# A scale from row sums on ScalarE, and three of six gates on ScalarE and GpSimd, at the seam of a fused block kernel

## The chip, the cores and the metric

The kernel runs on one core of a Trainium2 chip. A core has five engines with a queue of instructions each: TensorE (PE in the profile; its weight loads are PEld), VectorE (DVE), ScalarE (ACT), GpSimd (POOL) and SyncE (SP, which here issues the DMAs). Each engine takes its own queue in order; engines wait for each other through semaphores. The metric is the device time of one execution in microseconds; less is better.

## The reference

Three blocks follow each other on a batch of 4 sequences of 448 rows and 768 features. The cut below keeps what is computed.

```python
# attention with a sigmoid in place of the softmax; 12 heads of 64
scores = scale * q @ k.T - log(S)
x = sigmoid(scores) @ v                      # (4, 448, 768)

# Fourier mixing over rows and features, then a normed two-layer network
u = x + real(fft(fft(x, axis=1), axis=2))
un = (u - mean(u)) / sqrt(var(u) + 1e-6)
x = u + relu(un @ w_ch1) @ w_ch2             # 768 -> 3072 -> 768

# the convolution block: a causal 5-tap convolution per feature gates a projection
gate = sigmoid(sum_k conv_w[k] * x[:, s - 4 + k, :])
out = (gate * (x @ w_val)) @ w_out
```

## The kernel before

Features lie on the 128 partitions in 6 tiles, the 448 rows along the free axis; `acc[b]` holds one batch entry as 128 x 6 x (4 + 448) numbers in fp32 (four zeros of padding for the convolution). In the order of instructions the four are called `acc_90`, `acc_92`, `acc_94` and `acc_96`.

A product of fp32 matrices is made of three fp16 products: each operand is scaled by a power of two and split into a high and a low half. The scale needs the largest magnitude of a whole tensor, over all partitions. `peak` finds it: `peak_row` (lines 107 to 113) reduces a 128 x n tile of partial results to a column on DVE and spreads it to a diagonal `pd`; `peak_spread` (L118) lets PE multiply that by ones, which copies the column to all partitions; `peak_max` (L123) reduces it on DVE; `pow2` and `scaled` (L152 to L160) make the scale of it. **L118 is a matmul in PE's queue like any other: if `pd` isn't there, all of PE's later work waits.**

The code is a set of Python generators. What is recorded between two `yield`s goes to the engines' queues at that place of the program, and nothing is moved afterwards; so the place in the program is the place in each queue. PE's main work calls `background()` between pieces, which takes some steps of each list of side work: `wq` (weights: load, split into halves; then `prep_x2`), `lq`, `fq` (norms and the Fourier part), `gq` (`first_gates`).

The stages: (1) attention, 96 slots `t`, 24 for each batch entry (`r` counts them), with the weights of group 0 and the Fourier part and norm of earlier entries beside it. `amax_v` takes the largest magnitude of a tile of v on DVE, `peak_v` and `scale_v` make the scale that `fourier(b)` needs. (2) The two-layer network in 8 groups of 384 hidden features; block n is group n // 4 and batch entry n % 4. `up(n)` is 54 matmuls into PSUM tiles `ps_s` (two of them), which ACT (`hh`, L737) and DVE (`hl`, L739) evict; `down(n)` is 6 x 9 matmuls into `ps_m` tiles (four of them, taken in turn, L118's too), which DVE adds into `acc[b]` (L757). The blocks run up(n+1), down(n), up(n+2), and so on; the last are up(30), down(29), up(31), down(30), down(31). After down(28) `acc[0]` is final, and so on to `acc[3]` after down(31). (3) The convolution block: `prep_x2(b)` scales and splits `acc[b]` to fp16 halves `xs` (L795 on ACT, L797 on DVE), `first_gates` makes the six gates of entry 0 ahead of time, the other gates are made in the loop; `value` (L907) and `project` (L932) are 18 matmuls each.

Weights of a later block are loaded in halves: `HALF_AT` says at which group each of the four loads (`wv` twice, `wo` twice) is put in `wq`; `constants()` loads the convolution's taps `cw` behind them, and `prep_x2(0)` stands in `wq` behind that.

## Time and profile before

| what | value |
|---|---|
| time, median of 3 runs | 1113.61 us (1111.94 to 1113.67) |
| time of the profiled execution | 1113.55 us |
| its span in the trace | 1111.8 us |
| PE busy | 1066.1 us, 96% of the span |
| DVE, ACT, POOL busy | 756.1, 427.7 and 191.1 us |
| share of PE in the chain that ended last | 76%, DVE 16% |
| PE waiting at L118 | 19.6 us in 7 waits |

What lies around the span is 1113.55 - 1111.8 = 1.75 us. PE is the engine that sets the time wherever it is busy; the table is to be read for where it isn't. A slice of the page's second part is 27.8 us long: PE's busy digit falls below 8 in two slices only, the 35th and 36th of 40, where the granted clock falls too. That is the seam between the two-layer network and the convolution block.

### The profile page before, as it was taken

To read this page: it belongs to the slowest core of one execution; us is meant where nothing else is said; L and a number is where in the kernel's file an instruction comes from. 1 tells how busy PE (TensorE), PEld (TensorE's weight loads), DVE (VectorE), ACT (ScalarE), POOL (GpSimd) and SP (SyncE) were. 2 spreads that over 40 slices of the span, in tenths; PEclk is the share of its full clock that TensorE was granted. 3 is DMA by queue.
4 is the path that set the end of the run, shared out by engine and by line. 5 is a ranking of instruction groups with operands and counts; after the bars stand their busy time and mean duration, and the time that the engine had idled before them with its cause. 6 is when DMAs were issued, how large, how long until landed. Compare 5 with 4: busy or idle time off the path is not lost.

```text
span 1111.8 us, 15303 instructions
## 1 busy us (share of the span) xinstructions
PE 1066.1 (96%) x5616; PEld 550.7 (50%) x5616; DVE 756.1 (68%) x2154; ACT 427.7 (38%) x654; POOL 191.1 (17%) x171
## 2 busy tenths in 40 slices
PE   8899998989899999999999999999999967999998
PEld 4345453546455555555555555555555533555554
DVE  2866999697884676657676765676765679775530
ACT  5675656633232233333423233333233322343321
POOL 3322323331311111111101111110111100000000
PEclk9999999999999999999999999999999978999999
DMA  6723433011111322222333321233321100000001
GB/s 212 211 79 92 122 98 86 10 44 44 30 43 43 86 72 69 73 63 68 85 86 86 81 67 39 72 85 86 87 73 40 32 1 0 1 34 34 34 34 67
DMA packets 34780, 74.13 MB, mean 67 GB/s; under 512 B 3940, under 2 KB 11920, under 8 KB 34704
## 3 DMA queue, kind: packets, MB, share of 16 engines
q1 hardware_dynamic: 34704, 73.15, 23.2%
q8 instruction: 44, 0.72, 0.3%
q14 instruction: 32, 0.26, 0.1%
HBM read 67.46 MB, written 5.51 MB: 66 GB/s over the span
## 4 chain that ended last, share of the span: by engine, by line
PE 76%; DVE 16%; DMA 3%; ACT 3%; issue 1%; POOL 1%; SPq 0%; ACTq 0%; DVEq 0%; POOLq 0%
PE ps_s L730 26%; PE ps_m L753 26%; PE ps_m L932 7%; PE ps_m L907 7%; DMA w<-w1d 3%; PE ps_m L466 2%; PE ps_m L381 2%; PE ps_s L356 2%; PE ps_m L483 1%; DVE gp L820 1%; DVE wf L195 1%; DVE wf L198 1%; DVE xm L105 1%; DVE acc L757 1%; DVE wabs L190 1%
## 5 line engine op out<-in xcount | busy, mean ns | idle before, releaser
L730 PE MATMUL ps_s<-un,w1hi 128*128 128x448 f16 x1152 | 316.6, 357 | 3.5 <-DVE hl L739 3.5
L753 PE MATMUL ps_m<-hh,w2hi 128*128 128x448 f16 x576 | 205.1, 356 | 1.3 <-DVE acc L757 1.2
L730 PE MATMUL ps_s<-un,w1lo 128*128 128x448 f16 x576 | 205.5, 357 | 0.0
L753 PE MATMUL ps_m<-hl,w2hi 128*128 128x448 f16 x576 | 204.9, 356 | 0.0
L753 PE MATMUL ps_m<-hh,w2lo 128*128 128x448 f16 x576 | 204.7, 355 | 0.0
L730 PEld LDWEIGHTS <-w1hi 128*128 128x128 f16 x1152 | 113.5, 99 | 111.0 <-issue 8.8
L753 PEld LDWEIGHTS <-w2hi 128*128 128x128 f16 x1152 | 113.3, 99 | 108.5 <-issue 6.0
L757 DVE SCALAR_TENSOR_TENSOR acc<-ps_m,rg,acc 128x448 f32<-128x448 f32 x192 | 129.1, 678 | 41.8 <-PE ps_m L753 41.7
L179 ACT ACTIVATE wabs<-w 128x384 f32<-128x384 f32 (+1 forms) x109 | 58.4, 548 | 213.0 <-DMA w<-w2d 78.8
L739 DVE SCALAR_TENSOR_TENSOR hl<-ps_s,hh 128x896 f16<-128x896 f32 x64 | 54.6, 854 | 93.0 <-ACT hh L737 92.9
L190 DVE TENSOR_SCALAR_CACHE_REDUCE wabs<-wabs 128x192 f32<-128x192 f32 (+1 forms) x234 | 74.6, 353 | 35.9 <-ACT wabs L179 35.1
L369 ACT ACTIVATE sg<-ps_s,logb 128x896 f32<-128x896 f32 x96 | 86.3, 913 | 26.7 <-PE ps_s L356 22.4
L737 ACT ACTIVATE hh<-ps_s 128x896 f16<-128x896 f32 x64 | 46.2, 722 | 110.4 <-PE ps_s L730 110.4
L730 PEld LDWEIGHTS <-w1lo 128*128 128x128 f16 x576 | 56.9, 99 | 54.1 <-issue 2.5
L753 PEld LDWEIGHTS <-w2lo 128*128 128x128 f16 x576 | 56.8, 99 | 53.8 <-issue 2.0
L198 DVE SCALAR_TENSOR_TENSOR wf<-w,wf 128x192 int32<-128x192 int32 (+1 forms) x234 | 78.1, 371 | 0.3
L907 PE MATMUL ps_m<-xs,wvhi 128*128 128x448 f16 x288 | 78.0, 353 | 0.0
L195 DVE SCALAR_TENSOR_TENSOR wf<-w,wf 128x192 int32<-128x192 int32 (+1 forms) x234 | 77.0, 366 | 0.4
L192 DVE TENSOR_SCALAR wf<-wabs 128x192 int32<-128x192 int32 (+1 forms) x234 | 55.4, 275 | 31.7 <-POOL w1lo L231 12.7
L381 PE MATMUL ps_m<-sg,v 128*64 128x448 f32 x288 | 69.8, 564 | 0.0
L804 DVE SCALAR_TENSOR_TENSOR gp<-acc,cw,gp 128x448 f32<-128x448 f32 x72 | 49.3, 685 | 25.0 <-ACT gp L802 23.1
L932 PE MATMUL ps_m<-gh,wolo 128*128 128x448 f16 x144 | 50.8, 352 | 0.0
(187 smaller groups left out, 1398.4 us busy)
## 6 DMA issues: line engine op xcount, KB each, us to landing
w<-w1d SPq DMA_DIRECT2D x42, 384.0 KB
w<-w2d SPq DMA_DIRECT2D x42, 384.0 KB
k<-kd SPq DMA_DIRECT2D x24, 256.0 KB
v<-vd SPq DMA_DIRECT2D x24, 256.0 KB
q<-qd SPq DMA_DIRECT2D x24, 224.0 KB
out<-o SPq DMA_DIRECT2D x24, 224.0 KB
w<-wvd SPq DMA_DIRECT2D x12, 384.0 KB
w<-wod SPq DMA_DIRECT2D x12, 384.0 KB
```

The lines of the kernel that those rows point to most:

```text
L179: A.activation(out=wa, in_=z[:, :, 1].bitcast(F32), func=AF.Abs)
L190: V.tensor_scalar(out=a, in0=a, scalar1=LEAST, scalar2=None, op0=ALU.max, op1=ALU.max, accum_out=m[:, i:i + 1])
L192: V.tensor_scalar(out=f.bitcast(I32), in0=a.bitcast(I32), scalar1=0x07FFFFFF, scalar2=3, op0=ALU.bitwise_and, op1=ALU.logical_shift_left)
L195: V.scalar_tensor_tensor(out=f.bitcast(I32), in0=lo, scalar=29, in1=f.bitcast(I32), op0=ALU.logical_shift_right, op1=ALU.bitwise_or)
L198: V.scalar_tensor_tensor(out=f.bitcast(I32), in0=hi, scalar=-0x40000000, in1=f.bitcast(I32), op0=ALU.bitwise_and, op1=ALU.bitwise_or)
L369: A.activation(out=sg[:, :n], in_=sc.pop(t)[:, :n, :S], func=AF.Sigmoid, scale=1.0 / math.sqrt(D), bias=logb)
L381: nc.tensor.matmul(p[hs, :S], v[:, s, hs], a[:, h], start=(s == 0), stop=False)
L730: nc.tensor.matmul(p[:, i, :S], w[:, k, fs], u[:, k], start=(m == 0), stop=(m == 17))
L753: nc.tensor.matmul(p[:, :S], w[:, f, js], hh[f // 2][k][:, f % 2], start=(m == 0), stop=(m == 3 * FC - 1))
L757: V.scalar_tensor_tensor(out=acc[b][:, j, PAD:], in0=p[:, :S], scalar=rg, in1=acc[b][:, j, PAD:], op0=ALU.mult, op1=ALU.add)
L907: nc.tensor.matmul(p[:, :S], w[:, k, js], u[:, k], start=(n == 0), stop=(n == 17))
L932: nc.tensor.matmul(p[:, :S], w[:, k, js], gs[b, k][i], start=(n == 0), stop=(n == 17))
```

## The change

- `prep_x2`: the six DVE reductions to the largest magnitude (L105) are replaced by two ACT instructions (`Abs` over 3 x 448 elements each) whose accumulator gives the sum of magnitudes of a row. Their elementwise output goes to the place of the low halves, which L797 later overwrites. The scale's exponent `X2_EXP` goes from 12 to 14. `peak` now waits four steps between `peak_row` and L118, one step after it.
- `first_gates`: the gates are made in pairs (0,3), (1,4), (2,5). The first of a pair is made as before (ACT product, four DVE multiply-adds); of the second, ACT makes all five products (the last four into `gt`) and POOL adds them. The sigmoids come a pair later (`gate_ends`). `gq` gets one step of each `background()`, not two.
- The second half of `wo` is loaded from group 6 on, not 7, and `constants()` stands behind it in group 6.
- In attention, `amax_v` is called one tile ahead, and the three steps of `peak_v` stand at r = 19, 21 and 22 of the same entry, not at r = 23 and at 0 and 1 of the next. The last entry's steps after the loop are gone.
- The peak of the weights of group 0 waits four and two steps, not two and two.

```diff
-X2_EXP = 12
+X2_EXP = 14
-HALF_AT = (1, 3, 5, 7)
+HALF_AT = (1, 3, 5, 6)
...
-    def peak(m, nm, wait):
+    def peak(m, nm, wait, after=1):
         d = peak_row(m, nm)
         for _ in range(wait):
             yield
         p = peak_spread(d)
-        for _ in range(wait):
+        for _ in range(after):
             yield
         return peak_max(p, nm)
...
-        g = yield from (peak(m, nm, 2) if step == WCOLS else peak_pool(m, nm))
+        g = yield from (peak(m, nm, 4, 2) if step == WCOLS else peak_pool(m, nm))
...
-        if t % 4 == 2:
-            amax_v(b, r // 4)
-        if r == 23:
+        if t == 0:
+            amax_v(0, 0)
+        if t % 4 == 2 and t // 4 + 1 < NPAIR:
+            amax_v(*divmod(t // 4 + 1, NT))
+        if r == 19:
             peak_v(b, 0)
-        if b and r == 0:
-            peak_v(b - 1, 1)
-        if b and r == 1:
-            peak_v(b - 1, 2)
-            scale_v(b - 1)
+        if r == 21:
+            peak_v(b, 1)
+        if r == 22:
+            peak_v(b, 2)
+            scale_v(b)
...
-    peak_v(B - 1, 1)
     drain()
     finish(wq)
-    peak_v(B - 1, 2)
-    scale_v(B - 1)
...
     def prep_x2(b):
         xs = acc[b][:, :, PAD:]
-        m = keep.tile([128, NT], F32, tag="xm", bufs=2, name="xm")
-        for j in range(NT):
-            amax(xs[:, j], m, j)
-            if j % 2:
-                yield
-        g = yield from peak(m, "x2", 1)
+        xs2 = homes[b].tile([128, NT, 2 * S], F16, tag=f"un{b}", name="xs")
+        xh, xl = xs2[:, :, :S], xs2[:, :, S:]
+        m = keep.tile([128, 2], F32, tag="xm", bufs=2, name="xm")
+        for h in range(2):
+            hh = slice(3 * h, 3 * h + 3)
+            A.activation(out=xl[:, hh], in_=xs[:, hh], func=AF.Abs, accum_out=m[:, h:h + 1])
+            yield
+        yield
+        g = yield from peak(m, "x2", 4)
...
     def first_gates():
...
-        for j in range(NT):
-            gp = tt[:, j] if j < 4 else tw[:, (j - 4) * S:(j - 3) * S]
-            A.activation(out=gp, in_=acc[0][:, j, 0:S], func=AF.Copy, scale=cw[:, j, 0:1])
+        for pair in range(3):
+            js = pair, pair + 3
+            gp = tt[:, pair], tw[:, pair * S:(pair + 1) * S] if pair < 2 else tt[:, 3]
+            for j, g in zip(js, gp):
+                A.activation(out=g, in_=acc[0][:, j, 0:S], func=AF.Copy, scale=cw[:, j, 0:1])
             yield
             for k in range(1, 5):
-                V.scalar_tensor_tensor(out=gp, in0=acc[0][:, j, k:k + S], scalar=cw[:, j, k:k + 1], in1=gp, op0=ALU.mult, op1=ALU.add)
-                if k % 2 == 0:
-                    yield
-            for _ in range(3):
+                j, g = js[0], gp[0]
+                V.scalar_tensor_tensor(out=g, in0=acc[0][:, j, k:k + S], scalar=cw[:, j, k:k + 1], in1=g, op0=ALU.mult, op1=ALU.add)
+                j, g = js[1], gp[1]
+                A.activation(out=tp[:, n % 5], in_=acc[0][:, j, k:k + S], func=AF.Copy, scale=cw[:, j, k:k + 1])
+                P.tensor_tensor(out=g, in0=g, in1=tp[:, n % 5], op=ALU.add)
+                n += 1
                 yield
-            A.activation(out=gp, in_=gp, func=AF.Sigmoid)
-            gps[0, j] = gp
+            late.append((js, gp))
+            if pair:
+                gate_ends()
...
-        step(gq, 2)
+        step(gq)
...
-            if g == NG - 1:
+            if g == NG - 2:
                 wq.append(constants())
```

**The first peak of the seam, DVE and ACT.** DVE before, from the last of the constants to the first scale of `xs`; it stands in DVE's queue beside the evictions of down(29), and L118 follows on PE after 9 matmuls of up(31):

```order
L777 TENSOR_TENSOR evo_8459<-em,woe 128x1
L105 TENSOR_REDUCE xm<-acc_90 128x1 x2
L820 SCALAR_TENSOR_TENSOR gp<-acc_90,cw,gp 128x448 x2
L757 SCALAR_TENSOR_TENSOR acc_92<-ps_m,rg,acc_92 128x448
L105 TENSOR_REDUCE xm<-acc_90 128x1 x4
L820 SCALAR_TENSOR_TENSOR gp<-acc_90,cw,gp 128x448 x2
L110 TENSOR_REDUCE x2t<-xm 128x1
L112 TENSOR_SCALAR pd<-eye,x2t 128x128
L123 TENSOR_REDUCE x2g<-ps_m 128x1
```

DVE now, in the same place of the program's logic, which is one block and a half earlier; L118 follows on PE after 18 matmuls of down(29):

```order
L738 SCALAR_TENSOR_TENSOR hl<-ps_s,hh 128x896
L198 SCALAR_TENSOR_TENSOR cw<-w_8342,cw 128x30
L768 TENSOR_TENSOR em<-wve 128x1
...
L825 SCALAR_TENSOR_TENSOR gp<-acc_90,cw,gp 128x448
L738 SCALAR_TENSOR_TENSOR hl<-ps_s,hh 128x448
L110 TENSOR_REDUCE x2t<-xm 128x1
L112 TENSOR_SCALAR pd<-eye,x2t 128x128
L825 SCALAR_TENSOR_TENSOR gp<-acc_90,cw,gp 128x448
L756 SCALAR_TENSOR_TENSOR acc_92<-ps_m,rg,acc_92 128x448
L825 SCALAR_TENSOR_TENSOR gp<-acc_90,cw,gp 128x448
L756 SCALAR_TENSOR_TENSOR acc_92<-ps_m,rg,acc_92 128x448
```

ACT now, from the eviction of up(30) to the sigmoids of the first pair:

```order
L736 ACTIVATE hh<-ps_s 128x896
L821 ACTIVATE gp<-acc_90,cw 128x448 x2
L787 ACTIVATE xs,xm<-acc_90 128x3x448 x2
L827 ACTIVATE gt<-acc_90,cw 128x448
L736 ACTIVATE hh<-ps_s 128x448
L827 ACTIVATE gt<-acc_90,cw 128x448 x3
L795 ACTIVATE xs<-acc_90,sx 128x3x448 x2
L821 ACTIVATE gp<-acc_90,cw 128x448 x2
L827 ACTIVATE gt<-acc_90,cw 128x448 x3
L787 ACTIVATE xs,xm<-acc_92 128x3x448 x2
L827 ACTIVATE gt<-acc_90,cw 128x448
L840 ACTIVATE gp<-gp 128x448 x2
```

The six reductions are gone from DVE, and the magnitudes stand in ACT's queue behind the eviction of up(30) and the first products, ahead of the second `hh` of up(30). Four DVE multiply-adds of each pair are left, one between two evictions; POOL's queue has twelve `L828 TENSOR_TENSOR gp<-gp,gt` at its end and nothing beside them.

**The second peak and the evictions of down(30), DVE.** Before, around the same instructions for `acc[1]`:

```order
L105 TENSOR_REDUCE xm<-acc_92 128x1 x4
L110 TENSOR_REDUCE x2t<-xm 128x1
L112 TENSOR_SCALAR pd<-eye,x2t 128x128
L820 SCALAR_TENSOR_TENSOR gp<-acc_90,cw,gp 128x448 x2
...
L797 SCALAR_TENSOR_TENSOR xs<-acc_92,sx,xs 128x3x448
L820 SCALAR_TENSOR_TENSOR gp<-acc_90,cw,gp 128x448 x2
L757 SCALAR_TENSOR_TENSOR acc_94<-ps_m,rg,acc_94 128x448
L797 SCALAR_TENSOR_TENSOR xs<-acc_92,sx,xs 128x3x448
```

Now:

```order
L110 TENSOR_REDUCE x2t<-xm 128x1
L112 TENSOR_SCALAR pd<-eye,x2t 128x128
L825 SCALAR_TENSOR_TENSOR gp<-acc_90,cw,gp 128x448
L738 SCALAR_TENSOR_TENSOR hl<-ps_s,hh 128x896
...
L797 SCALAR_TENSOR_TENSOR xs<-acc_92,sx,xs 128x3x448
L825 SCALAR_TENSOR_TENSOR gp<-acc_90,cw,gp 128x448
L738 SCALAR_TENSOR_TENSOR hl<-ps_s,hh 128x448
L797 SCALAR_TENSOR_TENSOR xs<-acc_92,sx,xs 128x3x448
L825 SCALAR_TENSOR_TENSOR gp<-acc_90,cw,gp 128x448
L756 SCALAR_TENSOR_TENSOR acc_94<-ps_m,rg,acc_94 128x448 x6
```

All six evictions of down(30) now stand behind both L797 of entry 1 and the last of the gates' multiply-adds. L118 follows on PE after 36 matmuls of up(31).

**The end of attention, DVE.** Before, from the last norm of entry 1 to the first eviction of the network's first block:

```order
L617 TENSOR_TENSOR un<-tt,un 128x2x448
L399 TENSOR_TENSOR pm<-acc_96 128x448 x2
L123 TENSOR_REDUCE vg<-ps_m 128x1
L152 TENSOR_SCALAR ve<-vg 128x1
...
L426 TENSOR_TENSOR pm<-acc_96 128x448 x2
L190 TENSOR_SCALAR wabs,wm<-wabs 128x192 x2
L192 TENSOR_SCALAR wf<-wabs 128x192 x2
L430 TENSOR_TENSOR pm<-pm 128x3x223 x2
```

Now:

```order
L123 TENSOR_REDUCE vg<-ps_m 128x1
L152 TENSOR_SCALAR ve<-vg 128x1
...
L617 TENSOR_TENSOR un<-tt,un 128x2x448
L399 TENSOR_TENSOR pm<-acc_96 128x448 x2
L426 TENSOR_TENSOR pm<-acc_96 128x448 x2
L430 TENSOR_TENSOR pm<-pm 128x3x223 x2
L190 TENSOR_SCALAR wabs,wm<-wabs 128x192 x2
L192 TENSOR_SCALAR wf<-wabs 128x192 x2
```

The scale of v's last entry and the last norm of entry 1 stand ahead of the work that follows attention; on SP the DMAs of the Fourier part (L551, L408) now stand ahead of the weight loads, where before they stood behind them.

## Rows read from the trace of the kernel before

**Rows 1.** Stretches: start:end, length, then busy time (x instructions) of PE, PEld, DVE, ACT, POOL, PE's granted clock, DMA.
```profile
225.00:330.00 105.00, 94.09 (x504) 53.03 (x503) 91.75 (x240) 33.23 (x48) 29.77 (x24) 0.95 0.14 39
330.00:870.00 540.00, 539.25 (x2852) 278.85 (x2850) 355.03 (x1289) 174.96 (x280) 86.45 (x80) 1.00 0.27 72
870.00:945.00 75.00, 59.61 (x273) 28.83 (x272) 57.43 (x118) 23.30 (x31) 5.53 (x5) 0.86 0.00 1
```

**Rows 2.** PE's waits in the whole span: us in total, times, longest.
```profile
PE ps_m L118 <- DVE pd L112: 19.6, 7, 5.2
PE ps_s L730 <- DVE hl L739: 3.5, 1, 3.5
```

**Rows 3.** The chain that ended last, at up(30): start, us, engine, line.
```profile
868.75 10.21 PE ps_s L730 x54
```

**Rows 4.** Timeline of PE in the seam: start, us, instruction, [idle before <- releaser].
```profile
895.69 0.47 PE L118 MATMUL ps_m<-pd,ones_r 128*128 128x128 f32 x1 [4.82 <-DVE pd L112]
910.05 0.47 PE L118 MATMUL ps_m<-pd,ones_r 128*128 128x128 f32 x1 [4.80 <-DVE pd L112]
935.89 0.47 PE L118 MATMUL ps_m<-pd,ones_r 128*128 128x128 f32 x1 [5.22 <-DVE pd L112]
943.95 0.54 PE L907 MATMUL ps_m<-xs,wvhi 128*128 128x448 f16 x2
```

**Rows 5.** Timeline of DVE in the seam.
```profile
891.74 2.19 DVE L105 TENSOR_REDUCE xm<-acc 128x1 f32<-128x448 f32 x4
896.21 0.29 DVE L123 TENSOR_REDUCE x2g<-ps_m 128x1 f32<-128x128 f32 x1 [0.57 <-PE ps_m L118]
906.29 1.08 DVE L739 SCALAR_TENSOR_TENSOR hl<-ps_s,hh 128x896 f16<-128x896 f32 x1
909.91 1.40 DVE L820 SCALAR_TENSOR_TENSOR gp<-acc,cw,gp 128x448 f32<-128x448 f32 x2
920.44 0.68 DVE L757 SCALAR_TENSOR_TENSOR acc<-ps_m,rg,acc 128x448 f32<-128x448 f32 x1
940.53 3.14 DVE L797 SCALAR_TENSOR_TENSOR xs<-acc,sx,xs 128x1344 f16<-128x1344 f32 x2
```

**Rows 6.** Timeline of ACT in the seam.
```profile
897.29 2.72 ACT L795 ACTIVATE xs<-acc,sx 128x1344 f16<-128x1344 f32 x2 [9.46 <-DVE sx L160]
903.58 0.92 ACT L737 ACTIVATE hh<-ps_s 128x896 f16<-128x896 f32 x1 [2.54 <-PE ps_s L730]
926.50 0.58 ACT L825 ACTIVATE gp<-gp 128x448 f32<-128x448 f32 x1 [4.80 <-DVE gp L820]
926.98 0.65 ACT L817 ACTIVATE gp<-acc,cw 128x448 f32<-128x448 f32 x1
```

**Rows 7.** Timeline of POOL at the end of attention.
```profile
239.22 1.45 POOL L418 TENSOR_TENSOR pm<-pm 128x339 f32<-128x339 f32 x1 [0.79 <-DVE pm L430]
241.61 1.24 POOL L565 TENSOR_TENSOR tt<-tt,acc 128x448 f32<-128x448 f32 x1
```

**Rows 8.** Timeline of DVE at the end of attention.
```profile
230.15 1.08 DVE L617 TENSOR_TENSOR un<-tt,un 128x896 f16<-128x896 f32 x1
233.17 0.28 DVE L123 TENSOR_REDUCE vg<-ps_m 128x1 f32<-128x128 f32 x1
234.19 1.15 DVE L426 TENSOR_TENSOR pm<-acc 128x448 f32<-128x448 f32 x2
239.83 2.03 DVE L195 SCALAR_TENSOR_TENSOR wf<-w,wf 128x192 int32<-128x192 int32 x2
250.65 0.62 DVE L195 SCALAR_TENSOR_TENSOR wf<-w,wf 128x192 int32<-128x192 int32 x2
```

**Rows 9.** Two stretches of 2 us, columns as in the first group.
```profile
54.00:56.00 2.00, 0.87 (x3) 0.41 (x3) 1.93 (x7) 0.00 (x0) 0.00 (x0) 1.00 0.43 121
248.00:250.00 2.00, 2.00 (x7) 0.79 (x6) 1.63 (x8) 1.02 (x3) 0.00 (x0) 0.50 0.40 155
```

**Rows 10.** Timeline of PE in attention and at its end.
```profile
55.13 0.33 PE L118 MATMUL ps_m<-pd,ones_r 128*128 128x128 f32 x1 [2.52 <-DVE pd L112]
247.37 0.91 PE L730 MATMUL ps_s<-un,w1hi 128*128 128x448 f16 x2 [3.45 <-DVE hl L739]
```

More of the change, by code (lines that the diff above doesn't have):

```diff
@@ L782, in prep_x2 @@
         xs = acc[b][:, :, PAD:]
-        m = keep.tile([128, NT], F32, tag="xm", bufs=2, name="xm")
-        for j in range(NT):
-            amax(xs[:, j], m, j)
-            if j % 2:
-                yield
-        g = yield from peak(m, "x2", 1)
+        xs2 = homes[b].tile([128, NT, 2 * S], F16, tag=f"un{b}", name="xs")
[7 more added lines that the diff above has]
+        g = yield from peak(m, "x2", 4)
         e, i = pow2(g, "x2")
         sx = scaled(i, 2.0 ** X2_EXP, "sx")
-        xs2 = homes[b].tile([128, NT, 2 * S], F16, tag=f"un{b}", name="xs")
-        xh, xl = xs2[:, :, :S], xs2[:, :, S:]
         for h in range(2):
@@ L812, in first_gates, with gate_ends @@
         tw = wp.tile([128, NT, FG], F16, tag="w1hi", bufs=1, name="gp").rearrange("p a b -> p (a b)").bitcast(F32)
+        tp = wp.tile([128, 5, S], F32, tag="wf", bufs=1, name="gt")
+        n = 0
         while len(evo) < 2:
             yield
-        for j in range(NT):
-            gp = tt[:, j] if j < 4 else tw[:, (j - 4) * S:(j - 3) * S]
-            A.activation(out=gp, in_=acc[0][:, j, 0:S], func=AF.Copy, scale=cw[:, j, 0:1])
+        for pair in range(3):
[3 more added lines that the diff above has]
+                A.activation(out=g, in_=acc[0][:, j, 0:S], func=AF.Copy, scale=cw[:, j, 0:1])
             yield
             for k in range(1, 5):
-                V.scalar_tensor_tensor(out=gp, in0=acc[0][:, j, k:k + S], scalar=cw[:, j, k:k + 1], in1=gp, op0=ALU.mult, op1=ALU.add)
-                if k % 2 == 0:
-                    yield
-            for _ in range(3):
-                yield
-            A.activation(out=gp, in_=gp, func=AF.Sigmoid)
-            gps[0, j] = gp
+                j, g = js[0], gp[0]
[4 more added lines that the diff above has]
+                n += 1
+                yield
+            late.append((js, gp))
+            if pair:
+                gate_ends()
+    late = []
+    def gate_ends():
+        js, gp = late.pop(0)
+        for j, g in zip(js, gp):
+            A.activation(out=g, in_=g, func=AF.Sigmoid)
+            gps[0, j] = g
     NBLK = NG * B
@@ L889, in body @@
         step(gq)
+    gate_ends()
     wst.close()
```

## The prediction

> **What bounds the kernel now.** I read the busy time by stretches first: it tells where TensorE is the bound and where not. From 330 to 870 us PE is busy 539.25 of 540 us at a granted clock of 1.00, so nothing that only shortens other engines' work there can pay. From 870 to 945 it is busy 59.61 of 75, from 225 to 330 94.09 of 105 [rows 1]. PE's waits then say for what: 19.6 us in seven waits at L118, and one of 3.5 at L730 [rows 2]. The timeline has three of the seven in the seam, 4.82, 4.80 and 5.22, together 14.84 [rows 4]; 4.76 lie in attention.
>
> The seam in one sum: 54 matmuls of `up` take 10.21 [rows 3], 0.189 each, and a `down` has as many. From the start of up(30) at 868.75 [rows 3] to the first L907 at 943.95 [rows 4] there are five such blocks, 51.05 us. The stretch is 75.20 long, so 24.15 are lost: 14.84 in the three waits, 9.31 around them. Most of those 9.31 I put down to the clock, granted 0.86 in the mean [rows 1]. A wait of 3.45 at 247.37 [rows 10] was followed by two microseconds at 0.50, the 1.2 GHz level; one of 2.52 at 55.13 [rows 10] left the clock at 1.00 [rows 9]. A wait above some 3 us is thus paid more than once, one below 2.5 once.
>
> Why L118 waits: `pd` comes from DVE, whose queue holds six reductions of 0.55 each (2.19 for four), the gates' multiply-adds of 0.70 (1.40 for two) and evictions of 0.68 [rows 5], while PE comes to L118 only nine to 45 matmuls after the block before.
>
> **The change part by part: the seam.** Off DVE: three times six reductions, 18 x 0.55 = 9.9 us, and 12 of 24 multiply-adds, 12 x 0.70 = 8.4. On ACT: six `Abs`, and twelve more products at 0.48 from start to start [rows 6], 5.8. No row of before has an activation with an accumulator. L795 reads and writes as many elements in 1.36 (2.72 for two) [rows 6]: that is the lower bound, twice it the upper. I take 1.36, the row of the same shape. POOL's add of 128x448 fp32 took 1.24, the nearest dearer row 1.45 for 339 elements [rows 7]. I take 1.24.
>
> A multiply-add beside POOL isn't in the seam of before. At the end of attention L195, with two SBUF inputs, took 2.03 a pair while POOL ran, 0.62 without [rows 8]. So I let each L825 or L797 that meets an add wait for the add's end; bounds: nothing and a whole 1.24 each. L757, with an input in PSUM, I leave at 0.68.
>
> From here on L738, L756, L787, L825, L827, L828 and L928 are lines of the changed kernel (evictions `hl` and of `down`, `Abs`, multiply-add, product, POOL's add, the gated product). I replay the queues with these times, T = 0 at the first matmul of up(30).
> - First peak. The first 36 matmuls end at 6.8, `hh` (0.92 [rows 6]) at 7.8, `hl` (1.08 [rows 5]) at 8.9, `cw` at 9.1. ACT: two products to 10.3, two `Abs` to 13.1, a product to 13.6, the second `hh` to 14.1. DVE's L110 stands behind the second `hl` (14.8), so `pd` is there at 15.3. PE, 72 matmuls on, comes at 13.6: **wait 1.7**, where it was 4.82, and short enough for the clock.
> - down(29). Three L825 between the evictions each meet an add; L123 comes at 20.7 and PSUM tiles come late for PE by some 0.5. down(29) ends at 22.7, about 2.0 above 20.4 plus the 0.3 of L118.
> - Second peak. ACT, from `sx` at 21.75: two L795 to 24.5, five products, `Abs`. The last eviction of `acc[1]` is done at 30.8, the second `Abs` at 32.3, `pd` at 32.9. PE comes after 36 matmuls of up(31) at 29.5: **wait 3.4**, where it was 4.80. Here the clock may fall.
> - Evictions of down(30). They stand behind both L797 (1.57 each, 3.14 for two [rows 5]) and the last L825, so the first starts at about 47.6. PE wants its fifth PSUM tile at 45.5: **a new wait, about 2.8** with what follows. down(30) ends at 51.7.
> - down(31): 10.4. Its L118 comes after 36 matmuls with DVE free: **no wait**, where it was 5.22. End at 62.1.
>
> 75.2 - 62.1 = **13.1** less. With `Abs` at 1.8 and adds at 1.45 the same replay gives 9.8; with adds that block nothing, 16.6. The sigmoids (0.58 [rows 6]) are no more than before and come later, ahead of their use at L928 and later; they cost nothing, because `value` of entry 0 lies between, and 0.58 apiece if that cover goes. The half of `wo` that moves from group 7 to 6 costs nothing under a PE of 539.25 in 540; the tail after 945 keeps its instructions.
>
> **Attention and its end.** `pd` of v now has two slots instead of one between L112 and L118; of the 4.76 us I take 3.5 (bounds 0 and 4.76). At the end of attention L730 waits 3.45 at 247.37 [rows 10] for an `hl`; behind it the clock is at 0.50 [rows 9]. DVE's L617 (1.08) and the row from L123 at 233.17 to L426 at 234.19 (1.02) [rows 8] move ahead of that, 2.1 us of DVE. DVE is busy 91.75 of 105 there [rows 1], so it is the bound. Against it, on SP the Fourier part's DMAs now stand ahead of the weight loads, and `prep` of the weights may be late for it. Ends: 6.9 (wait, the clock after it, 1.2 of small waits) and -2. I take 2.5, near the 2.1 that leave DVE's path.
>
> Sum: 13.1 + 3.5 + 2.5 = 19.1. The profiled execution took 1113.55, the median is 1113.61, so its sum stands for both: 1113.55 - 19.1 = 1094.5.
>
> **A rule against it.** The pair of L195 at 2.03 against 0.62 [rows 8] shows DVE held up while POOL works. The Trainium skill, "SBUF — State Buffer", section "SBUF: two separate sides", says that the port pair which the two share is an exclusive lock for a whole instruction, taken by a DVE operation with two SBUF inputs against a GpSimd operation that reads SBUF; by it the trace agrees, and L825 and L797 are of that kind. The Trainium skill, "Perfetto Trace Analysis", section "Optimizing Scalar/DVE Operations", says that moving work between these two engines might not help for this reason. By that rule the 8.4 us of multiply-adds save nothing; taken off the sum in full it would be 10.7, and the time 1102.9. The rows of POOL's side bear it out only in part, since half of the moved work are products, which go to ACT.
>
> **The rivals.**
> - R1, the adds hold nothing up. Speaks for it: L757 reads PSUM, and POOL waits for ACT's products as often as it runs. Seam 16.6: 1090.9; with the whole 6.9 at attention's end 1086.5. Chance 0.13.
> - R2, the seam pays, but the early 6.0 don't: waits in the first 330 us come back elsewhere, since DVE has 91.75 of 105 anyway [rows 1]. 1113.55 - 13.1 = 1100.4; 1104 if the seam is at its lower bound of 9.8. Chance 0.20.
> - R3, ACT becomes the seam's bound: with an accumulator an `Abs` costs 2.72, and the second `hh` and then `pd` come 2.7 later at each of the first two peaks: 5.4, more with the clock. 1094.5 + 5.4 = 1099.9, up to 1106. Against it: ACT is busy 23.30 of 75 [rows 1]. Chance 0.10.
> - R4, slower: POOL's lock takes DVE. Each of 12 L825 and six L797 waits a whole add: 18 x 1.24 = 22.3, of which the replay has some 5.3. 17.0 more against 13.1 saved, the evictions and `sx` late by it, and the early gain gone: 1117.4. It decides once the lock costs over 13 us more than I hold on DVE's path. Against it: only twelve adds, 14.9 us of POOL in all. Chance 0.08.
> - R5, the change doesn't do what it says: L118 is late by what stands ahead of it whoever sums, its wait goes from DVE's queue to ACT's. About 1113.6. Against it: DVE loses 18.3 us of work in the seam and ACT has room. Chance 0.06.
>
> **How the numbers follow.** My forecast, 1094.5, has 0.43. Its own spread is 1090 to 1099. The range goes from 1087 (R1 with the full gain) to 1106 (R3's end, R2 within it) and leaves out R4 and R5, 0.14, and some of the ends. Two in a thousand, 2.2 us, is about what a measurement of this kernel can tell. Forecast, R1, R2 and R3 are faster by more: 0.86. Same is R5, 0.06; slower R4, 0.08.
>
> **What would show it.** L118's waits in the seam: 1.7, 3.4 and none, against 4.82, 4.80 and 5.22; a wait of PE at down(30)'s fifth tile for L756; L787 at 1.36; L828 at 1.24, with L825 at 0.70 outside it and up to 1.9 beside it; the first L907 some 62 us after up(30) began; L118 in attention under 1.3 in all, and L729's wait near 247 shorter. I'm wrong if `Abs` is far dearer, if L825 or L797 stretch without bound, if the clock falls in the seam though no wait is above 2.5, or if PE's waits before 330 sum to what they were.

## The result, and the profile after

The changed kernel takes 1096.33 us in the median of four runs (1094.29 to 1096.84); beside it the kernel before took 1113.64. The ratio is 0.985, with a 95% interval of 0.983 to 0.987: faster by 1.5%, where 1.7% was forecast (1094.5 us, range 1087 to 1106). The profiled execution took 1096.84 with a span of 1095.1, so the span is 1111.8 - 1095.1 = 16.7 shorter, against 19.1 in the prediction's sum.

The busy time by stretches of the changed kernel, in the columns of [rows 1]; the last row is the seam itself, from the first matmul of up(30) to the first of `value`:

```profile
225.00:330.00 105.00, 93.23 (x498) 52.60 (x497) 84.86 (x219) 32.51 (x48) 32.00 (x24) 0.97 0.15 43
330.00:870.00 540.00, 540.00 (x2856) 279.36 (x2855) 355.90 (x1305) 180.77 (x289) 89.55 (x84) 1.00 0.27 72
...
864.41:926.51 62.10, 53.84 (x274) 27.18 (x273) 40.86 (x69) 32.28 (x49) 21.52 (x16) 0.97 0.00 1
```

The same seam in the kernel before:

```profile
868.58:943.95 75.37, 59.98 (x274) 29.02 (x273) 57.56 (x119) 23.86 (x32) 5.53 (x5) 0.86 0.00 1
```

The seam is 75.37 - 62.10 = 13.27 shorter. Up to its start the changed kernel is 868.58 - 864.41 = 4.17 ahead. Behind it, from the first matmul of `value` to the end, it needs (1095.1 - 926.51) - (1111.8 - 943.95) = 0.74 more. 4.17 + 13.27 - 0.74 = 16.70. In the seam PE's waits went from 15.32 to 8.23, 7.09 less; 6.14 more are PE's busy time, 59.98 to 53.84, for the same 274 matmuls at a granted clock of 0.86 before and 0.97 now.

Those of PE's waits in the whole span that bear on the change, as in [rows 2] (releaser, us in total, times, longest):

```profile
PE ps_m L752 <- DVE acc L756: 4.3, 1, 4.3
PE ps_s L729 <- DVE hl L738: 4.2, 1, 4.2
PE ps_m L118 <- DVE pd L112: 3.9, 2, 2.6
...
PE ps_m L923 <- DVE gp L928: 0.7, 1, 0.7
```

L118 went from 19.6 in seven waits to 3.9 in two. The timeline of PE, which answers to [rows 4] and [rows 10], tells where (start, us, instruction, idle before and releaser):

```profile
227.96 0.54 PE L729 MATMUL ps_s<-un,w1hi 128*128 128x448 f16 x2
...
243.26 0.91 PE L729 MATMUL ps_s<-un,w1hi 128*128 128x448 f16 x2 [4.16 <-DVE hl L738]
...
879.51 0.33 PE L118 MATMUL ps_m<-pd,ones_r 128*128 128x128 f32 x1 [1.32 <-DVE pd L112]
...
896.26 0.33 PE L118 MATMUL ps_m<-pd,ones_r 128*128 128x128 f32 x1 [2.60 <-DVE pd L112]
...
911.13 0.35 PE L752 MATMUL ps_m<-hh,w2hi 128*128 128x448 f16 x1 [4.31 <-DVE acc L756]
...
922.87 0.38 PE L118 MATMUL ps_m<-pd,ones_r 128*128 128x128 f32 x1
...
926.51 0.54 PE L923 MATMUL ps_m<-xs,wvhi 128*128 128x448 f16 x2
```

Three waits of 4.8 to 5.2 became 1.32, 2.60 and none, and a new one of 4.31 stands at the fifth tile of down(30). Attention ends at 227.96, where it ended at 231.29 before, and no L118 waits in it. DVE in the seam, as in [rows 5]:

```profile
879.37 1.56 DVE L825 SCALAR_TENSOR_TENSOR gp<-acc,cw,gp 128x448 f32<-128x448 f32 x1
...
881.45 0.95 DVE L825 SCALAR_TENSOR_TENSOR gp<-acc,cw,gp 128x448 f32<-128x448 f32 x1
...
897.75 0.69 DVE L825 SCALAR_TENSOR_TENSOR gp<-acc,cw,gp 128x448 f32<-128x448 f32 x1 [1.55 <-ACT gp L821]
...
907.23 1.79 DVE L797 SCALAR_TENSOR_TENSOR xs<-acc,sx,xs 128x1344 f16<-128x1344 f32 x1
908.94 1.54 DVE L825 SCALAR_TENSOR_TENSOR gp<-acc,cw,gp 128x448 f32<-128x448 f32 x1
910.41 2.45 DVE L756 SCALAR_TENSOR_TENSOR acc<-ps_m,rg,acc 128x448 f32<-128x448 f32 x4
```

The multiply-add L825 takes 0.69 where POOL is still and 0.95 to 1.56 where an add runs. The four evictions that PE waits for start at 910.41, at once behind L797 and L825. ACT, as in [rows 6], in the seam and at the end of attention:

```profile
239.93 1.36 ACT L260 ACTIVATE e<-eo,st 12x452 f16<-12x452 f32 x2 [5.66 <-DVE eo L419]
241.19 0.89 ACT L736 ACTIVATE hh<-ps_s 128x896 f16<-128x896 f32 x1
...
876.03 1.31 ACT L787 ACTIVATE xs<-acc 128x1344 f16<-128x1344 f32 x1
877.25 0.19 ACT L787 ACTIVATION_READ_ACCUMULATOR xs<-acc 128x1 f32 x1
```

And POOL's adds, as in [rows 7], of the first pair:

```profile
878.07 5.34 POOL L828 TENSOR_TENSOR gp<-gp,gt 128x448 f32<-128x448 f32 x4 [5.77 <-ACT gt L827]
```

### The profile page after: what moved, and what is told of

Same layout as the page of the kernel before. It is cut to its first block, busy times and chain, and to the rows that moved or that the text cites. A ratio compares the mean times of both kernels' runs of the same rounds, so it can differ in the third digit from the quotient of the medians.

```text
span 1095.1 us, 15323 instructions
## 1 busy us (share of the span) xinstructions
PE 1061.2 (97%) x5616; PEld 550.0 (50%) x5616; DVE 736.5 (67%) x2118; ACT 444.6 (41%) x682; POOL 209.4 (19%) x183
## 4 chain that ended last, share of the span: by engine, by line
PE 75%; DVE 17%; ACT 4%; DMA 2%; issue 1%; POOL 0%; SPq 0%; DVEq 0%; POOLq 0%; ACTq 0%
PE ps_m L752 27%; PE ps_s L729 26%; PE ps_m L948 7%; PE ps_m L923 6%; PE ps_s L356 2%; PE ps_m L381 2%; PE ps_m L466 2%; DMA w<-w1d 2%; PE ps_m L483 1%; DVE gp L804 1%; DVE hl L738 1%; DVE pm L430 1%; DVE gp L825 1%; DVE xs L797 1%; PE ps_m L383 1%
## 5 line engine op out<-in xcount | busy, mean ns | idle before, releaser
L729 PE MATMUL ps_s<-un,w1hi 128*128 128x448 f16 x1152 | 312.8, 353 | 4.2 <-DVE hl L738 4.2
L752 PE MATMUL ps_m<-hh,w2hi 128*128 128x448 f16 x576 | 204.0, 354 | 4.3 <-DVE acc L756 4.3
L752 PE MATMUL ps_m<-hh,w2lo 128*128 128x448 f16 x576 | 203.9, 354 | 0.0
L752 PE MATMUL ps_m<-hl,w2hi 128*128 128x448 f16 x576 | 203.9, 354 | 0.0
L752 PEld LDWEIGHTS <-w2hi 128*128 128x128 f16 x1152 | 112.7, 98 | 109.8 <-issue 6.2
L752 PEld LDWEIGHTS <-w2lo 128*128 128x128 f16 x576 | 56.6, 98 | 53.1 <-issue 0.9
L923 PE MATMUL ps_m<-xs,wvhi 128*128 128x448 f16 x288 | 78.0, 352 | 0.7 <-DVE gp L928 0.7
L195 DVE SCALAR_TENSOR_TENSOR wf<-w,wf 128x192 int32<-128x192 int32 (+1 forms) x234 | 75.8, 362 | 0.3
L948 PE MATMUL ps_m<-gl,wohi 128*128 128x448 f16 x144 | 50.8, 352 | 0.3 <-DVE gl L932 0.3
```

The lines of the kernel that those rows point to most:

```text
L195: V.scalar_tensor_tensor(out=f.bitcast(I32), in0=lo, scalar=29, in1=f.bitcast(I32), op0=ALU.logical_shift_right, op1=ALU.bitwise_or)
L729: nc.tensor.matmul(p[:, i, :S], w[:, k, fs], u[:, k], start=(m == 0), stop=(m == 17))
L752: nc.tensor.matmul(p[:, :S], w[:, f, js], hh[f // 2][k][:, f % 2], start=(m == 0), stop=(m == 3 * FC - 1))
L923: nc.tensor.matmul(p[:, :S], w[:, k, js], u[:, k], start=(n == 0), stop=(n == 17))
L948: nc.tensor.matmul(p[:, :S], w[:, k, js], gs[b, k][i], start=(n == 0), stop=(n == 17))
```

## The experiments

The sum came out right in the seam. The question was whether it was right for its reason. The change has four parts there that the runs take apart: the sums of magnitudes on ACT (Abs), three gates on ACT and POOL (split), the earlier place of the half of `wo`, the constants and with them `prep_x2(0)` (place), and four steps instead of one between `pd` and L118 (distance). My theory was that DVE's relief, the first two, pays; the rivals were place and distance. Diffs are against the changed kernel unless said. "Seam" is always the time from the first matmul of up(30) to the first of `value`; "waits" are PE's in it.

| run | sums | gates | place | steps to L118 | seam | waits | PE busy | DVE busy | time | ratio to before (95%) |
|---|---|---|---|---|---|---|---|---|---|---|
| before | DVE | DVE | late | 1 | 75.37 | 15.3 | 59.98 | 57.56 | 1113.64 | |
| changed kernel | ACT | split | early | 4 | 62.10 | 8.2 | 53.84 | 40.86 | 1096.33 | 0.983 to 0.987 |
| gates on DVE | ACT | DVE | early | 4 | 59.06 | 4.6 | 54.45 | 42.70 | 1094.86 | 0.980 to 0.984 |
| maxima on DVE | DVE | split | early | 4 | 60.80 | 5.9 | 54.90 | 47.88 | 1096.92 | 0.982 to 0.985 |
| both on DVE | DVE | DVE | early | 4 | 62.67 | 8.4 | 54.30 | 51.70 | 1098.77 | 0.982 to 0.987 |
| late place | ACT | split | late | 4 | 57.68 | 3.9 | 53.68 | 40.71 | 1095.12 | 0.979 to 0.985 |
| L118 soon | ACT | split | early | 1 | 61.71 | 6.3 | 55.37 | 42.45 | 1095.35 | 0.980 to 0.985 |
| before, distance alone | DVE | DVE | late | 4 | 69.50 | 12.5 | 56.99 | 54.71 | 1108.33 | 0.993 to 0.996 |
| no adds | ACT | adds left out | early | 4 | 56.13 | 4.0 | 51.99 | 36.21 | 1092.68 | 0.979 to 0.982 |
| gates on DVE, far | ACT | DVE | early | 8 | 56.37 | 4.1 | 52.28 | 41.40 | 1092.26 | 0.977 to 0.981 |
| gates on DVE, late, far | ACT | DVE | late | 6 | 59.60 | 4.7 | 54.91 | 43.24 | 1093.97 | 0.979 to 0.984 |

How far a seam of the same code varies: two pairs of kernels have it in common. The changed kernel and the one with attention put back have 62.10 and 60.41; the two runs on the low halves, further below, have 60.00 and 58.57. Each row of the table is one profiled execution, beside the median time of four runs or more. So differences below some 1.7 in the seam say nothing, and as two pairs are few, one a little above counts only where the times agree. Each ratio is to runs of the kernel before that were made beside that kernel; their medians are 1113.64 to 1114.96.

### Three gates back on DVE

```
-                A.activation(out=tp[:, n % 5], in_=acc[0][:, j, k:k + S], func=AF.Copy, scale=cw[:, j, k:k + 1])
-                P.tensor_tensor(out=g, in0=g, in1=tp[:, n % 5], op=ALU.add)
+                V.scalar_tensor_tensor(out=g, in0=acc[0][:, j, k:k + S], scalar=cw[:, j, k:k + 1], in1=g, op0=ALU.mult, op1=ALU.add)
```

> All six first gates on DVE again (24 multiply-adds), places, sums of magnitudes and attention as in the changed kernel. In the trace of the changed kernel the twelve L825 and four L797 of the seam are 4.6 us longer than alone (0.69 and 1.57 each), which I lay to POOL's adds; twelve more L825 are 8.4. My theory: DVE has 8.4 - 4.6 = 3.8 more on its path, the third wait (4.31 in the changed kernel, for L756 in down(30)) grows by about that, seam 66 (64.5 to 68) against 62.1, time about 1100. Rival, the lock eats what POOL takes: seam 62.1 within 0.7, no L825 above 0.75.

Measured: seam 59.06, shorter than with the split, and 1094.86 us. PE's timeline and the seam's row:

```profile
897.90 0.47 PE L118 MATMUL ps_m<-pd,ones_r 128*128 128x128 f32 x1 [3.85 <-DVE pd L112]
```
```profile
865.48:924.54 59.06, 54.45 (x275) 27.52 (x274) 42.70 (x81) 25.57 (x37) 4.97 (x4) 0.94 0.00 1
```

The second wait is longer (3.85 for 2.60), and the one of 4.31 in down(30) is gone. DVE has twelve multiply-adds more and is busy 1.84 longer. My theory (66) falls; the rival has the direction, but its bound (0.7 around 62.1) was too high as well. The split saves nothing that can be seen here, in the seam or in the time (1094.86 against 1096.33).

### Maxima back on DVE

```
-            hh = slice(3 * h, 3 * h + 3)
-            A.activation(out=xl[:, hh], in_=xs[:, hh], func=AF.Abs, accum_out=m[:, h:h + 1])
+            for j in range(3 * h, 3 * h + 3): amax(xs[:, j], m, j)
```

> The six maxima of each entry on DVE again (6 x 0.55 = 3.3 us), at the place where ACT's Abs stand now; gates split as in the changed kernel. My theory: at the first peak nothing changes (DVE has room before the second hl, wait 1.3 as now); at the second they follow the last eviction of acc[1], pd is there some 2.6 later, wait 5.2 instead of 2.6 with a fall of the clock, evictions of down(30) later by as much: seam 68 (65 to 71), time 1102. Rival, it is the earlier place in the queues that pays and not the engine: seam 62 to 63.

```profile
899.10 0.48 PE L118 MATMUL ps_m<-pd,ones_r 128*128 128x128 f32 x1 [4.67 <-DVE pd L112]
```

The second wait grew as expected (4.67; 5.2 was expected), but the seam is 60.80, within the spread of 62.10: the third wait is gone here too. PE begins down(30) 40.2 us after up(30) where it was 35.4, and DVE's first eviction of down(30) starts at 44.5 where it was 46.0: DVE isn't later there for its six reductions, and PE, held at L118, no longer comes before the evictions. **When DVE is late for both, PE pays the lateness once, at the first place where it meets it.** That is the step that my theory had left out.

### Both back on DVE: place and distance alone

The two diffs above together.

> Both back on DVE: maxima and all six gates; what stays of the change is the place (half of wo and constants from group 6, four steps between pd and L118, one step of the gates' list) and attention. My theory (engines matter): DVE carries 9.9 + 8.4 - 4.6 = 13.7 us more in the seam than in the changed kernel, about half of it on the path: seam 70 (67 to 74), time 1104. Rival, place alone: seam at most 64, time at most 1098.5. Rival, place is worth nothing: seam 75, time 1109.5.

```profile
880.73 0.33 PE L118 MATMUL ps_m<-pd,ones_r 128*128 128x128 f32 x1 [1.36 <-DVE pd L112]
...
901.76 0.47 PE L118 MATMUL ps_m<-pd,ones_r 128*128 128x128 f32 x1 [7.01 <-DVE pd L112]
```
```profile
865.58:928.25 62.67, 54.30 (x274) 27.42 (x273) 51.70 (x99) 17.64 (x25) 4.98 (x4) 0.95 0.00 1
```

Seam 62.67, time 1098.77: the rival "place alone" holds (seam at most 64, and 0.3 above its time of 1098.5), and my theory (70) falls. DVE does 10.8 us more in the same seam, and PE pays one wait of 7.01 in place of 2.60 and 4.31.

### Late place

```
-HALF_AT = (1, 3, 5, 6)
+HALF_AT = (1, 3, 5, 7)
...
-            if g == NG - 2:
+            if g == NG - 1:
                 wq.append(constants())
```

(`gt` is allocated behind the constants, since the half of `wo` still uses its memory.)

> Engines as in the changed kernel (Abs on ACT, three gates on ACT and POOL), the second half of wo from group 7 and constants behind it, as before the change; so prep of acc[0] stands about a block and a half later. My theory (engines matter more than place): the peaks' data is ready as fast as in the changed kernel after each entry is final, so waits at L118 of 1 to 3 each, but the work of three entries falls nearer together and behind down(31): seam 66 (63 to 69), time 1100. Rival, place is all: seam 73 to 75, time 1107 to 1109.

```profile
901.73 0.33 PE L118 MATMUL ps_m<-pd,ones_r 128*128 128x128 f32 x1 [2.49 <-DVE pd L112]
```
```profile
864.95:922.63 57.68, 53.68 (x274) 27.16 (x273) 40.71 (x86) 34.20 (x52) 21.25 (x17) 0.97 0.01 1
```

Seam 57.68, shorter than in the changed kernel, so "place is all" falls as well. With the engines relieved the early place isn't needed; in this run no L752 waits in the seam, where the changed kernel has 4.31. That it is better than early isn't shown: the profiled execution took 1092.94, where the four runs go from 1091.58 to 1099.07, and the medians, 1095.12 and 1096.33, differ by 1.2.

### L118 soon, and distance alone

With neither engines nor place decisive, distance was the next theory. From both sides: one step in the changed kernel, and four steps in the kernel before.

```
-        g = yield from peak(m, "x2", 4)
+        g = yield from peak(m, "x2", 1)
```

> The changed kernel with one step instead of four between the entry's pd (L112) and L118; all else, engines and places, as in the changed kernel. New theory (distance): what paid in the seam is that PE comes to L118 some 18 matmuls (3.4 us) later after the row that makes pd, not which engine sums. Then the waits at L118 are 3.4 longer, about 4.7, 6 and 2.5, the clock falls after the first two, and the wait of 4.31 in down(30) goes into them: seam 70 (66 to 74) against 62.1, time 1104. Rival (engines or place): seam within 1.5 of 62.1.

```profile
880.89 0.33 PE L118 MATMUL ps_m<-pd,ones_r 128*128 128x128 f32 x1 [3.02 <-DVE pd L112]
...
912.11 0.35 PE L752 MATMUL ps_m<-hh,w2hi 128*128 128x448 f16 x1 [2.23 <-DVE acc L756]
```

Seam 61.71: the distance theory falls in this direction (66 to 74 was expected). The first wait is 1.7 longer, the later ones shorter: the second `pd` is there 31.8 us after up(30) began in both kernels, and PE, held up at the first, comes later to the second. The test is weaker than was meant, though: the edit moves each L118 by 9 matmuls, 1.7 us, and not by the 18 expected; in the other direction it is 18, 27 and 9. Against the kernel before:

```
-        g = yield from peak(m, "x2", 1)
+        g = yield from peak(m, "x2", 4)
```

> The kernel before with one edit: four steps instead of one between the entry's pd and L118, one after it as before. Maxima and all gates on DVE, places, attention, two steps of the gates' list: all as before. Distance theory: waits of 4.82, 4.80 and 5.22 become about 1.4, 1.4 and 1.8, the clock stays: seam 62 (59 to 65) against 75.4 before, time 1100.5. Rival (the engines are needed): DVE is as full as before, the waits only move to L753 or L907: seam 72 to 75, time 1110 to 1113.6.

```profile
896.03 0.33 PE L118 MATMUL ps_m<-pd,ones_r 128*128 128x128 f32 x1 [1.40 <-DVE pd L112]
911.16 0.47 PE L118 MATMUL ps_m<-pd,ones_r 128*128 128x128 f32 x1 [6.27 <-DVE pd L112]
...
931.85 0.47 PE L118 MATMUL ps_m<-pd,ones_r 128*128 128x128 f32 x1 [4.31 <-DVE pd L112]
```
```profile
868.93:938.43 69.50, 56.99 (x274) 28.14 (x273) 54.71 (x117) 21.43 (x30) 5.54 (x5) 0.90 0.01 1
```

The first wait became 1.40, as expected, but the next two are 6.27 and 4.31: seam 69.50, 5.9 gained where 13 was expected. Distance moves a wait; as long as DVE has 55 us of work crowded there, the next peak meets it.

The reliefs are thus substitutes for the most part. Distance alone gives 5.9. With distance, the early place gives 6.8 more (69.50 to 62.67), the engines give 11.8 (69.50 to 57.68), and both together give 7.4 (69.50 to 62.10). By the median times (1108.33, 1098.77, 1095.12, 1096.33, the first without the gain in attention) both together are as good as the engines within the spread; what is clear is that they are far from 6.8 + 11.8. With each of the three come the gates in pairs and one step of their list instead of two, which no run here takes apart; engines alone or place alone, with one step to L118, were not run either.

One reading holds the nine kernels together that have the early place and at most four steps (some of them follow below). From PE's first matmul on down(30)'s fifth tile, the row of L752 at 911.13 in the changed kernel, to the first of `value` it is 13.7 to 13.8 us in six of them, and 15.1 to 15.4 in the three in which the clock falls to 0.50 around that matmul. The rest of the difference is when PE gets there: 42.4 to 48.9 us after up(30) began. In some it waits there for DVE's evictions, in the others it comes late from L118. So a part of the change pays only as far as it lets PE get to that matmul sooner.

### The adds left out

```
-                P.tensor_tensor(out=g, in0=g, in1=tp[:, n % 5], op=ALU.add)
```

> POOL's twelve adds (L828) are left out, all else as in the changed kernel; three of the six first gates then lack four of five taps. It prices what the adds cost DVE. My theory: L825 all at 0.69 and L797 at 1.57, 4.6 us less on DVE's path; the wait of 4.31 in down(30) falls to 1 to 2.5 without a fall of the clock after it, the wait of 2.60 at the second L118 to about 1.5: seam 57.5 (56 to 59.5), time about 1092. Rival, what DVE loses to POOL is hidden: seam 62.1 within 0.7.

DVE's timeline, PE's, and the seam's row:

```profile
893.71 1.40 DVE L825 SCALAR_TENSOR_TENSOR gp<-acc,cw,gp 128x448 f32<-128x448 f32 x2
```
```profile
909.06 0.35 PE L752 MATMUL ps_m<-hh,w2hi 128*128 128x448 f16 x1 [2.69 <-DVE acc L756]
```
```profile
866.62:922.75 56.13, 51.99 (x274) 26.69 (x273) 36.21 (x69) 32.28 (x49) 4.98 (x4) 1.00 0.00 1
```

Nearly as expected: L825 takes 0.67 to 0.70 throughout, DVE is busy 40.86 - 36.21 = 4.65 less without having less to do, the wait in down(30) is 2.69 (1 to 2.5 was expected), that at the second L118 is 0.12 (1.5), and the clock stays at 1.00. The adds cost the seam 4.3 to 6.0 (60.41 and 62.10 against 56.13), and 3.7 by the median times. The rival, that what DVE loses is hidden, falls.

### Attention put back

```
-        if r == 19:
+        if r == 23:
             peak_v(b, 0)
-        if r == 21:
-            peak_v(b, 1)
-        if r == 22:
-            peak_v(b, 2)
-            scale_v(b)
+        if b and r == 0:
+            peak_v(b - 1, 1)
+        if b and r == 1:
+            peak_v(b - 1, 2)
+            scale_v(b - 1)
```

(`amax_v` and the steps after the loop likewise.)

> Attention as before the change (amax_v not ahead, peak_v at r = 23, 0, 1, scale of the last entry after the loop); weights' peak and the seam as in the changed kernel. In the changed kernel attention ends 3.3 us earlier and the stretch behind it gives 0.85 more. My theory: both come from these edits: 4.2 back, time 1100.5, L118 waiting 4.5 us in attention again, seam 62.1 as it is. Rival, the early gain would be given back elsewhere: time within 1 of the changed kernel's.

1100.72 us (ratio 0.986 to 0.990 to before), 4.4 above the changed kernel; attention ends at 231.37, up(30) starts at 869.95, and L118 waits 6.4 in all, 2.5 of it in attention, where 4.5 was expected. The early gain comes from these edits and isn't given back; that all of it is L118's waits isn't shown.

### The low halves later, and the work on r later

To see whether the rest of the seam can be had, the low halves (L797) of an entry were made behind the next entry's `pd`; in a second run the work on `r` in the last Fourier part also stands three steps later.

```
-            V.scalar_tensor_tensor(out=xl[:, hh], in0=xs[:, hh], scalar=sx, in1=xh[:, hh], op0=ALU.mult, op1=ALU.subtract)
+        lows_of.append(V.scalar_tensor_tensor(out=xl[:, i:i + 3], in0=xs[:, i:i + 3], scalar=sx, in1=xh[:, i:i + 3], op0=ALU.mult, op1=ALU.subtract) for i in (0, 3))
...
-            for _ in range(2):
+            for _ in range(2 if b < B - 1 else 5):
```

> The low halves (L797) of an entry are made one entry later, behind that entry's pd, so that neither the evictions of down(29) and down(30) nor the second hl of up(31) stand behind them. My theory, DVE's order is what is left in the seam: wait at the second L118 0 to 0.5 (from 2.60), wait in down(30) 0 to 1 (from 4.31), no fall of the clock: seam 53.5 (52.5 to 56), the time 1088.5. Rival, DVE's total work binds: the 3.2 us an entry come back as waits of L923 or L948 after the seam, time within 2 of the changed kernel's.

Seam 60.00, time 1096.40: no gain. DVE's timeline, then ACT's:

```profile
897.38 4.01 DVE L797 SCALAR_TENSOR_TENSOR xs<-acc,sx,xs 128x1344 f16<-128x1344 f32 x2
...
909.19 0.62 DVE L738 SCALAR_TENSOR_TENSOR hl<-ps_s,hh 128x448 f16<-128x448 f32 x1 [3.18 <-ACT hh L736]
```
```profile
905.46 2.72 ACT L795 ACTIVATE xs<-acc,sx 128x1344 f16<-128x1344 f32 x2 [5.45 <-DVE sx L160]
```

The two L797 (4.01 beside POOL) now delay L123 and `sx`; ACT's L795 waits for `sx`, the last `hh` of up(31) stands behind it, and DVE's `hl` and evictions wait for that. The time that my theory gave DVE back was lost through ACT's queue. The rival's time came (1096.40, within 2 of 1096.33), but only a part of it by its way: behind the seam L948 waits 1.35, 1.06 more than in the changed kernel.

> As the run with the low halves later, and in the last Fourier part the work on r (L446, L447, and e on ACT) stands three steps later, behind the first hh and hl of up(0). In the changed kernel PE waits 4.16 there for an hl, which waits for hh, which stands on ACT behind e (L260), which waits for DVE's L419. My theory: that wait falls to 1 to 2 and the clock stays, 3 us (1 to 4.5) less than the run without this edit. Rival: the Fourier part is bound by the same DVE work, and the time comes back as waits of L466, L483 or L596 before 330 us: within 0.7 of it.

PE's waits from 225 to 330 us in that run:

```profile
PE ps_m L596 <- DVE tt L588: 6.0, 2, 3.1
...
PE ps_s L729 <- DVE hl L738: 1.4, 1, 1.4
```

The wait at the end of attention fell from 4.2 to 1.4, and L596 waits 6.0 where it waited 1.9 in the changed kernel and in the run without this edit. up(30) starts at 866.39, against 866.27 without it, and the time is 1097.58, 1.2 above (0.7 was the rival's bound). My theory (3 less) falls; that the wait comes back at L596, as the rival had it, is shown.

### A faster version

All first gates on DVE, and eight steps between `pd` and L118; then the same with the late place and six steps.

```
-        g = yield from peak(m, "x2", 4)
+        g = yield from peak(m, "x2", 8)
```

> The changed kernel with all six first gates on DVE (nothing on POOL) and eight steps between pd and L118. Distance theory: the waits of the run with gates on DVE, 0.76 and 3.85, become 0 and 0.5, without a fall of the clock; evictions of down(30) come ahead of L797: seam 53.5 (52 to 56), time 1088.5. Rival (DVE's whole work binds): sx and the low halves come so late that L923 or L948 waits, and what the seam gains is lost behind it: time within 2 of 1094.9.

```profile
899.59 0.33 PE L118 MATMUL ps_m<-pd,ones_r 128*128 128x128 f32 x1 [0.44 <-DVE pd L112]
906.47 0.35 PE L752 MATMUL ps_m<-hh,w2hi 128*128 128x448 f16 x1 [1.44 <-DVE acc L756]
```
```profile
867.17:923.54 56.37, 52.28 (x274) 26.68 (x273) 41.40 (x76) 26.51 (x39) 4.98 (x4) 1.00 0.00 1
```

1092.26 us, ratio 0.979 (0.977 to 0.981): below the changed kernel's interval. Against the run with gates on DVE and four steps (0.980 to 0.984) the gain isn't clear of the spread. The waits at L118 are as expected; four short ones at L752, the longest 1.44, stand in their place, so the seam is 56.4 and not 53.5. The clock is granted 1.00 throughout the seam. The rival's waits behind the seam didn't come: none is left there.

> As the run with late places (half of wo from group 7, constants behind it), but all six first gates on DVE and six steps between pd and L118; of the change there stay Abs on ACT, the distance and attention. Distance theory: waits 0, 0.8 and 0 instead of 0, 2.49 and 1.36: seam 54 (52.5 to 57), time 1089.5, about as the run with early places and eight steps. Rival (the late place crowds DVE at the end of the seam): L923 waits for gates of entry 0 or for xs, time 1093 to 1097.

Seam 59.60, 1093.97 us. The second wait is 2.21 and one of 1.45 follows it in down(30). The theory's waits (0, 0.8, 0) didn't come. Nor did the rival's: L923 waits 0.69, as it does in the changed kernel (0.68). The time is in the rival's range all the same, for the waits inside the seam.

## Why the prediction was right, and where it wasn't

**The seam's size: right, and the last digit by luck.** The replay gave 62.1; the trace has 62.10, where the same code took 60.41 with attention put back. Its stations hold as well, counted from the first matmul of up(30): first wait 1.32 (1.7 forecast), L123 at 20.0 (20.7), end of down(29) at 22.3 (22.7), second wait 2.60 with the clock kept (3.4, where it might fall). In down(30) the evictions start at 46.0 (47.6) and PE comes earlier than I had it, at 42.4 (45.5), so the new wait is 4.31 and not 2.8. The evictions were 1.6 early, and behind the wait the clock fell, which the replay hadn't and which costs 1.4 to 1.7 there: the two errors cancel. L787 takes 1.31 and 0.19 for the accumulator, not twice 1.36, so R3 didn't come; L828 takes 1.33 in a row of four and 1.13 alone (1.24).

**The seam's reason: wrong in its weights.** "Off DVE: 18 x 0.55 = 9.9 us, and 12 x 0.70 = 8.4" is true as a count, and the replay, which took the new place and the new distance for granted, added it up. But with both parts undone the seam is 62.67. What I missed was a rival: that the edits of place and distance would do it without the engines. R5, the nearest, had only a wait that goes from one queue to another. The cost of a part can't be read off a sum in which the other parts already stand.

**POOL's lock: rather too small.** I let it cost the seam 16.6 - 13.1 = 3.5; leaving the adds out shows 4.3 to 6.0, with a spread of 1.7. The 8.4 of moved multiply-adds bring nothing that the runs show (59.06 without the split). The row of L195 [rows 8] pointed there, and here L825 shows it, 0.69 alone and up to 1.56 beside an add. The sentence in the Trainium skill, "Perfetto Trace Analysis", section "Optimizing Scalar/DVE Operations", that moving work between these two engines might not help, agrees with this trace.

**Attention: right in size, in part by luck.** 3.5 was forecast; attention ends 3.33 earlier, and the run with it put back gives 3.4. L118's waits there went from 4.51 to none (of the prediction's 4.76, 0.27 lie behind the seam, at 951.20), and all of PE's waits there from 14.5 to 8.9. But PE is busy 218.65 us of attention where it was 216.53: its granted clock, 1.00 before, now stands at 0.50 from 39 to 41 us and from 186 to 188:

```profile
39.00:41.00 2.00, 2.00 (x10) 0.79 (x8) 1.85 (x6) 2.00 (x5) 1.15 (x1) 0.50 0.63 194
```

So 3.33 is what was left of some 5.6, and the end of attention varies among traces of the same code: 227.76 to 229.86 in the ten that share the first 330 us with the changed kernel, 231.29 and 230.00 in the two that share it with the kernel before.

**The end of attention: little, where 2.5 was forecast.** In this trace 4.17 - 3.33 = 0.84 are left for it. From the end of attention to up(30) it is 636.4 to 639.3 us in the ten traces, 637.3 in the mean, and 637.3 and 638.9 in the two: 0.8 in the mean, less than the spread. The step that failed is "2.1 that leave DVE's path": DVE's path did get shorter, L419 starts 11.6 us after the end of attention where it was 14.1; but ACT's `hh` had moved behind `e` (L260, which starts at 239.93, released by L419), and `hl` waits for `hh`, so PE waits 4.16 for the same DVE work through another queue. The order showed it on ACT, which I hadn't laid beside DVE there.

**The tail: 0.74 lost, where nothing was forecast.** Two waits, at L923 (0.68) and at L948 (0.29), are new against 0.27 before.

## What to carry to other kernels

When an engine is late and another waits for it at several points, a wait at the first point can cover the next: relief at one point then shows up as a wait at the next, and several reliefs are substitutes, not terms of a sum. That holds as long as no new late work comes in between; before the change, and with distance alone, each of three entries brought its own. Price a part of a change by taking it alone out of the finished kernel and alone into the old one. Work moved from DVE to POOL isn't saved where POOL's runs meet DVE operations with two SBUF operands: here twelve adds cost DVE 4.65 us.
